# A decode block with grouped attention and a gated layer: the first weight's leading columns are loaded by a transfer of 112 rows and one of 16 rows

## The chip, the cores and the metric

The kernel runs on one core of a Trainium2 chip. A core has five engines with instruction streams of their own (PE or TensorE for matrix products, DVE or VectorE, ACT or ScalarE, POOL or GpSimd, SP or SyncE, which here only issues transfers) and 16 DMA engines that carry the transfers between HBM and the on-chip SBUF. The metric is the device time of one execution in microseconds (us), as a median of several.

## The reference

A layer norm of x, attention of one new token against cached keys and values, a bilinear gated layer, and their product added to x. Cut to what matters:

```python
B, Sq, D = 2, 1, 448
Hq, Hkv, Sk, Dh = 16, 8, 4096, 256      # two query heads share one key/value head
F = 1792

def reference(A_x, A_k_cache, A_v_cache, A_wq, A_wo, B_x, B_w_gate, B_w_up, B_w_down):
    xn = _layernorm(A_x, axis=-1)
    q = (xn @ A_wq).reshape(B, Sq, Hq, Dh).transpose(0, 2, 1, 3)
    k = jnp.repeat(A_k_cache, 2, axis=1)
    v = jnp.repeat(A_v_cache, 2, axis=1)
    p = softmax(jnp.einsum("bhqd,bhkd->bhqk", q, k) * Dh ** -0.5)
    o = jnp.einsum("bhqk,bhkd->bhqd", p, v)
    s = o.transpose(0, 2, 1, 3).reshape(B, Sq, Hq * Dh) @ A_wo
    g = silu((xn @ B_w_gate) * (xn @ B_w_up) @ B_w_down)
    return A_x + s * g
```

All is float32. The caches hold 2 x 8 x 4096 x 256 values each, 134 MB together; the weights add 24 MB. Each byte is read once.

## The kernel before, in words

All inputs are laid out by the host as arrays of 128 rows, one for each SBUF partition, so that each load is one transfer of 128 long rows. `gated_decode_block` keeps three large places in SBUF: a ring of two buffers of 128 x 16384 values (`ring`), and one buffer `slot`. A list `todo`, filled by `plan`, names what is loaded into which place and in which order: w_q's first half (`wq0`, 128 x 7168, into the front of the second ring buffer), the gate and up weights together (`wgu`, first ring buffer), down weights with w_q's second half (`wdq`, slot), the keys of the first pair (`first`, behind wq0 in the second ring buffer), then for each of the 16 pairs of head and batch the values of one pair with the keys of the next (`vk`), `wo` into the slot on the way, and at the end `last0` and `last1`, the second one cut into pieces of 6144, 2048, 2240, 896 and 448 columns. `issue(n)` takes the next n entries of the list and puts one `dma_start` on SP for each piece (`SP.dma_start(t[:, lo:hi], src[:, lo:hi])`, line 272). `issue(4)` at line 291 puts out the first four before anything else.

The order of work on each engine is the order in which the program calls them. A recorder, `Flow`, keeps every call with the boxes of tensors that it reads and writes, and `settle` works out from these which earlier operations it has to wait for; each transfer that somebody waits for has a semaphore of its own. SP works through its transfers in order; a `vk` transfer waits until PE has done with the ring buffer that it overwrites. The two rows of x are loaded by two transfers of one row each on ACT's queue (line 300).

Compute follows the loads: the layer norm of x, `query(0)` (w_q's first half), `ffn_in` (gate and up), `ffn_out` (down), `query(1)`, then a loop over seven pairs of pairs with scores, softmax and values, and an end part in which the last pair is attended, the heads are combined and projected with `wo` and with `wo2`, the three short pieces at the end of `last1` (`project_last`), multiplied by the gate, added to x and stored by one transfer (`res`).

`rows(ps, w, n)` multiplies xn with a folded weight: for k in 0 to 2 and c in 0 to 3 it takes the block of n columns number 4 k + c. For `wq0` n is 512, so that the first four matmuls use columns 0 to 2047, and the others the columns behind.

Of the kernel before, what the change touches and what calls it, by code (L numbers as in the profile page):

```python
# [22 lines left out]
EPS = 1e-5  # L23
WQ = 14 * 512
LEAD = 48


class Flow:
# [115 lines left out]
    def issue(self):  # L144
        nc = self.nc
        lead = nc.alloc_semaphore("lead")
        for _ in range(LEAD):
            nc.vector.sem_inc(lead)
# [72 lines left out]
        return add  # L221


def gated_decode_block(nc, x, first, vk, last0, last1, wq0, wdq, wo, wgu, out):
    flow = Flow(nc)
    PE, DVE, ACT, POOL, SP = [getattr(flow, e) for e in ("PE", "DVE", "ACT", "POOL", "SP")]
    names = iter(range(1000))
# [32 lines left out]
    loaded = {}  # L260
    todo = []

    def issue(n=1):
        for names, place, src, cuts in todo[:n]:
            t = place()
            width = ROW if not names[0].startswith("w") else src.shape[1] // len(names)
            for i, name in enumerate(names):
                loaded[name] = t[:, i * width:(i + 1) * width]
            if names == ["wd", "wq1"]:
                loaded["wd"], loaded["wq1"] = t[:, :14 * D], t[:, 14 * D:]  # L270
            for lo, hi in zip(cuts, cuts[1:]):
                SP.dma_start(t[:, lo:hi], src[:, lo:hi])
        del todo[:n]
# [15 lines left out]
    plan(f"k{LAST + 1} v{LAST}", ring, last0, [0, ROW, 2 * ROW])  # L289
    plan(f"v{LAST + 1} wo2", ring, last1, [0, 6144, ROW, *(ROW + i * D for i in (5, 7, 8))])  # L290
    issue(4)


# [230 lines left out]
    for first in range(0, LAST, B):  # L524
        flow.turn = first
        issue(2)
        if first == 0:
            flow.turn = None
            issue()
            flow.turn = first  # L530
        for i in range(first, first + B):
            p = softmax(i, s)
            o = bank("o")
            values(i, p, o)
            DVE.tensor_copy(ob[:, i % B], o)
            q = copy()
            POOL.tensor_copy(q, query_of(i + 1))
            s = scores(i + 1, q, two())
        total(add_head)
        cb = combine(ob)  # L540
        t = work["h"]()[:, :B * 64]
        DVE.tensor_tensor(t.rearrange("p (s k) -> p s k", s=B), cb.rearrange("p (s k) -> p s k", s=B),
                          over[:, :, None].to_broadcast([128, B, 64]), op=OP.mult)
        turn(oT, first // B, t)
# [19 lines left out]
    t = work["h"]()  # L564
# [62 lines left out]
```

## Time and profile before

| | |
|---|---|
| median of 3 runs | 374.37 us (374.28 to 374.49) |
| the profiled execution's own time | 374.30 us |
| its span in the profile | 372.7 us |
| bytes moved | 158.67 MB, mean 426 GB/s |

The span runs from the first to the last recorded instruction of the profiled execution; 1.6 us of its own time lie around it. In the views below, "SPq" is SP issuing a transfer, PEld the loading of weights into TensorE, and a line like `o<-ring,pT` names what is written and what is read. L220 is the line of the recorder through which nearly all instructions pass, so that operations are told apart by the tensors they touch. A view by stretches gives, for each stretch in us from the span's start, its length, the busy time of PE, PEld, DVE, ACT and POOL with the number of instructions, the granted clock of TensorE, the mean busy share of the 16 DMA engines and the GB/s they moved. A line of a DMA queue gives packets, MB and the share of the 16 engines' time. A line of DMA issues gives the number of issues, KB each and the median time in us from issue to landing. A timeline's line has the start, the duration, the instruction and in brackets how long its engine stood idle before and what ended that.

### The profile page before, as it was taken

The page shows a single profiled execution, that of the slowest core. Times are in us where ns is not written, and L with a number is a line of the kernel's source. Part 1 is how long each engine was busy: PE and PEld are TensorE (multiplying, and loading weights), DVE is VectorE, ACT ScalarE, POOL GpSimd, SP SyncE. Part 2 cuts the span into 40 slices and gives each one's busy share as a digit, 9 for nine tenths or more (in the row PEclk, how much of TensorE's full clock was granted, in tenths as well). Part 3 has the DMA queues.
Part 4 walks back from the last instruction along what each step waited for, and adds up shares of the span by engine and source line. Part 5 has one row for each costly group of instructions (what it writes and reads, how often), then busy time and mean ns, then how long its engine had stood idle before and what let it go on. Part 6 is the DMA issues. An engine that isn't in the chain of part 4 may idle for free. (4 is left out here: it accounts for less than half of the span.)

```text
span 372.7 us, 3346 instructions
## 1 busy us (share of the span) xinstructions
PE 188.0 (50%) x1474; PEld 57.2 (15%) x1474; DVE 75.5 (20%) x124; ACT 26.7 (7%) x44; POOL 5.6 (2%) x28
## 2 busy tenths in 40 slices
PE   0818292171900626555453638271919090908786
PEld 0201020020200201111121102020202030202223
DVE  2101013021130030313031212221131304030430
ACT  1101011001010010101000000101010101010121
POOL 0100000000000000000000000000000000000000
PEclk9968598596875685958595958695867586776999
DMA  8999999999999999999999999999999999999995
GB/s 339 466 424 410 429 433 450 443 445 396 425 459 436 450 443 436 429 394 450 436 450 443 436 429 394 450 436 450 443 436 429 394 450 436 450 397 443 421 414 233
DMA packets 3897, 158.67 MB, mean 426 GB/s; under 512 B 562, under 2 KB 692, under 8 KB 820
## 3 DMA queue, kind: packets, MB, share of 16 engines
q1 hardware_dynamic: 3888, 158.59, 98.6%
q8 instruction: 4, 0.07, 0.1%
q14 instruction: 1, 0.01, 0.0%
q10 hardware_dynamic: 4, 0.00, 0.0%
HBM read 158.54 MB, written 0.06 MB: 426 GB/s over the span
## 5 line engine op out<-in xcount | busy, mean ns | idle before, releaser
L220 PE MATMUL o<-ring,pT 128*32 128x512 f32 x480 | 81.4, 840 | 115.3 <-PEq L172 115.3
L220 PE MATMUL s<-ring,qc 128*32 128x512 f32 x448 | 50.7, 592 | 0.0
L220 PEld LDWEIGHTS o<-ring,pT 128*32 128x32 f32 x480 | 20.7, 149 | 163.5 <-issue 163.5
L220 DVE COPY ob<-o 128x512 f32<-128x512 f32 x14 | 9.7, 692 | 155.9 <-PE o L220 155.9
L220 ACT ACTIVATE p<-s,m 128x1024 f32<-128x1024 f32 x16 | 17.8, 1113 | 287.5 <-DVE m L220 287.5
L220 DVE TENSOR_REDUCE m<-s 128x1 f32<-128x1024 f32 x16 | 19.3, 1205 | 21.9 <-PE s L220 21.9
L220 DVE STREAM_TRANSPOSE pT<-p 128x1024 f32<-128x1024 f32 x15 | 18.7, 1245 | 19.1 <-ACT p L220 19.1
L220 PEld LDWEIGHTS s<-ring,qc 128*32 128x32 f32 x448 | 15.1, 110 | 33.0 <-issue 33.0
L220 PE MATMUL sm<-ident,m 128*1 128x128 f32 x16 | 4.3, 269 | 25.6 <-PEq L172 23.7
L220 PE MATMUL s<-ring,xnT 128*32 128x448 f32 (+1 forms) x72 | 12.1, 828 | 8.3 <-DMA ring<-wgu 8.3
L220 DVE TENSOR_REDUCE mx<-sm 1x128 f32<-1x512 f32 x16 | 10.9, 679 | 8.0 <-PE sm L220 8.0
L220 PE MATMUL sm<-one,mx 1*128 1x1 f32 x16 | 3.2, 198 | 12.9 <-PEq L172 12.1
L220 PE MATMUL s<-slot,hT 128*32 128x448 f32 x28 | 5.4, 885 | 8.0 <-DMA slot<-wdq 8.0
L220 POOL COPY qc<-qT 128x64 f32<-128x64 f32 x14 | 3.2, 236 | 290.9 <-PE s L220 283.6
L220 PE MATMUL s<-ring,qT 128*32 128x512 f32 x64 | 7.5, 597 | 0.0
L220 PEld LDWEIGHTS sm<-ident,m 128*1 128x1 f32 x16 | 1.3, 79 | 35.1 <-issue 32.9
L220 DVE RECIPROCAL over<-sm 128x2 f32<-128x2 f32 x8 | 1.4, 170 | 23.9 <-PE sm L220 23.9
L220 PE MATMUL s<-ident,pT 2*128 2x2 f32 x4 | 0.6, 247 | 10.5 <-DVE pT L220 10.5
L220 PE MATMUL cb<-ob,add_blocks 128*32 128x128 f32 x128 | 5.2, 279 | 0.6 <-ACT ob L220 0.6
L220 PEld LDWEIGHTS s<-ring,xnT 128*32 128x32 f32 x72 | 2.6, 145 | 17.0 <-DMA ring<-wgu 9.2
L220 PE MATMUL s<-ring,oT 128*32 128x112 f32 (+2 forms) x76 | 5.1, 314 | 0.1
L220 PE MATMUL wide<-slot,oT 128*32 128x448 f32 x48 | 4.9, 539 | 0.0
(65 smaller groups left out, 60.9 us busy)
## 6 DMA issues: line engine op xcount, KB each, us to landing
ring<-last SPq DMA_DIRECT2D x2, 4096.0 KB, 26.3
slot<-wdq SPq DMA_DIRECT2D x1, 6720.0 KB, 42.2
ring<-wgu SPq DMA_DIRECT2D x1, 6272.0 KB, 26.0
slot<-wo SPq DMA_DIRECT2D x1, 5376.0 KB, 46.6
ring<-first SPq DMA_DIRECT2D x1, 4096.0 KB, 51.2
ring<-wq SPq DMA_DIRECT2D x1, 3584.0 KB, 11.7
ring<-last SPq DMA_DIRECT2D x1, 3072.0 KB, 21.1
ring<-last SPq DMA_DIRECT2D x1, 1120.0 KB, 23.7
```

Source lines behind the costliest of these rows:

```text
L220: self.flow.record(self.engine, lambda: method(out, *args, **kw), writes, reads, name == "dma_start")
```

## The change

The first 2,048 of wq0's 7,168 columns become two arrays of their own: `wqs` with rows 0 to 111, and `wqx` with rows 112 to 127, stored as 4 groups of 4 rows with an unused fifth row behind each group, which keeps the groups from lying end to end. Three transfers take the place of one: 112 rows of 8,192 bytes, then 16 rows of 8,192 bytes whose source is the 4 x 4 pattern, then 128 rows of the 5,120 columns left. All three go to the places in SBUF where the one transfer went.

```diff
+SHARE = 4
+EACH = 4
+COLS = 2048
...
-def gated_decode_block(nc, x, first, vk, last0, last1, wq0, wdq, wo, wgu, out):
+def gated_decode_block(nc, x, first, vk, last0, last1, wq0, wqs, wqx, wdq, wo, wgu, out):
...
+            if names == ["wq0"]:
+                most = 128 - SHARE * EACH
+                loaded["wq0"] = t[:, :WQ]
+                SP.dma_start(t[:most, :COLS], wqs)
+                SP.dma_start(t[most:, :COLS], wqx[:, :EACH])
+                SP.dma_start(t[:, COLS:WQ], src)
+                continue
...
+    most = 128 - SHARE * EACH
+    wqs = c(wq0[:most, :COLS])
+    wqx = np.zeros((SHARE, EACH + 1, COLS), np.float32)
+    wqx[:, :EACH] = wq0[most:, :COLS].reshape(SHARE, EACH, COLS)
+    wq0 = c(wq0[:, COLS:])
```

On SP, at the head of its queue (each row names the place that is written, the array that is read, and the shape), before:

```order
L220 DMA ring<-wq 128x7168
L220 DMA ring<-wgu 128x12544
L220 DMA slot<-wdq 128x13440
L220 DMA ring<-first 128x8192
L220 DMA ring<-vk 128x16384 x2
```

and now, three lines further down in the file:

```order
L223 DMA ring<-wqs 112x2048
L223 DMA ring<-wqx 16x1x2048
L223 DMA ring<-wq 128x5120
L223 DMA ring<-wgu 128x12544
L223 DMA slot<-wdq 128x13440
L223 DMA ring<-first 128x8192
L223 DMA ring<-vk 128x16384 x2
```

wgu, wdq and first have two more issues ahead of them; all later transfers stand as before.

On PE, from the first matmul of query(0) to the first of ffn_in (xnT and the part of oT named here hold the transposed xn; s0, s1 and so on are semaphores), before:

```order
L220 MATMUL s<-ring,xnT 32x512 [waits s7,s0]
L220 MATMUL s<-ring,xnT 32x512
L220 MATMUL s<-ring,xnT 32x512 [waits s7]
L220 MATMUL s<-ring,xnT 32x512 x9
L220 MATMUL s<-ring,oT 64x512 x2
L220 MATMUL s<-ring,xnT 32x448 [waits s9,s1]
```

and now:

```order
L223 MATMUL s<-ring,xnT 32x512 [waits s9,s1,s0]
L223 MATMUL s<-ring,xnT 32x512
L223 MATMUL s<-ring,xnT 32x512 [waits s9]
L223 MATMUL s<-ring,xnT 32x512
L223 MATMUL s<-ring,xnT 32x512 [waits s2]
L223 MATMUL s<-ring,xnT 32x512 x7
L223 MATMUL s<-ring,oT 64x512 x2
L223 MATMUL s<-ring,xnT 32x448 [waits s11,s3]
```

The first matmul waits for the two small transfers (s0, s1) instead of the whole weight, and the fifth for the rest (s2). The number and order of the matmuls is the same; the numbers of the other semaphores move up by two.

More of the change, by code (lines that the diff above doesn't have):

```diff
@@ L619 @@
     nc = bacc.Bacc("TRN2", target_bir_lowering=False, num_devices=1, dynamic_dma_scratch_size=1024)
-    arrays = dict(x=x, first=first, vk=vk, last0=last[0], last1=last[1], wq0=wq0, wdq=wdq, wo=wo, wgu=wgu)
+    arrays = dict(x=x, first=first, vk=vk, last0=last[0], last1=last[1], wq0=wq0, wqs=wqs, wqx=wqx, wdq=wdq, wo=wo, wgu=wgu)
     args = [nc.dram_tensor(n, a.shape, mybir.dt.from_np(a.dtype), kind="ExternalInput").ap()
```

## The prediction

> **What bounds the kernel now.** I read the page first: span, busy shares, the DMA queues, and the chain that ended last.
>
> ```profile
> span 372.7 us, 3346 instructions
> ...
> PE 188.0 (50%) x1474; PEld 57.2 (15%) x1474; DVE 75.5 (20%) x124; ACT 26.7 (7%) x44; POOL 5.6 (2%) x28
> ...
> q1 hardware_dynamic: 3888, 158.59, 98.6%
> q8 instruction: 4, 0.07, 0.1%
> q14 instruction: 1, 0.01, 0.0%
> q10 hardware_dynamic: 4, 0.00, 0.0%
> ...
> DMA 6%; PE 3%; DVE 0%; issue 0%
> DMA ring<-last 6%; PE o L220 2%; PE s L220 1%; DVE gate L220 0%
> ```
>
> No compute engine is busy for more than half of the span, while the sixteen DMA engines spend 98.6% of it on SP's queue (q1). The kernel is a stream of weights and caches, and it ends when the last piece has come in. The next view is the DMA queue between 60 and 340 us, away from start and end.
>
> ```profile
> q1 hardware_dynamic: 2174, 121.34, 100.0%
> ```
>
> There the engines have no gap: 121.34 MB in 280 us are 433 GB/s, or 27.1 GB/s for each of 16 engines. Such a stream has no meeting point: an engine that loses a microsecond early carries the loss to the end, as long as the next transfer is always issued before the engine needs it. Whether it is, the issue table says.
>
> ```profile
> ring<-wq SPq DMA_DIRECT2D x1, 3584.0 KB, 11.7
> ...
> ring<-vk SPq DMA_DIRECT2D x14, 30.0
> ```
>
> A vk transfer of 8.39 MB takes 19.4 us at 433 GB/s but lands 30.0 us after its issue, so it stands in the queue for some 10.6 us before its turn. An engine may run several microseconds ahead of or behind the others without meeting an empty queue. So the end is not set by the mean of the engines but by the slowest of them, and the stretches at the end show whether they finish together (the columns wanted are the last two: DMA share and GB/s).
>
> ```profile
> 367.00:368.00 1.00, 0.44 (x16) 0.38 (x16) 0.00 (x0) 0.51 (x1) 0.00 (x0) 1.00 0.97 375
> 368.00:368.50 0.50, 0.43 (x17) 0.22 (x13) 0.22 (x1) 0.00 (x0) 0.00 (x0) 1.00 0.50 190
> 368.50:369.00 0.50, 0.50 (x32) 0.50 (x28) 0.09 (x1) 0.00 (x0) 0.00 (x0) 1.00 0.29 115
> 369.00:369.50 0.50, 0.50 (x24) 0.27 (x18) 0.00 (x0) 0.00 (x0) 0.00 (x0) 1.00 0.22 86
> 369.50:370.00 0.50, 0.50 (x20) 0.31 (x21) 0.00 (x0) 0.00 (x0) 0.00 (x0) 1.00 0.00 0
> ```
>
> They do not. All are busy until 368; after 368.5 a share of 0.29, then 0.22, is left: 115 and 86 GB/s are 4.2 and 3.2 engines at 27.1. So about four engines run until about 369.5 and twelve have stopped soon after 368. The three shares times 0.5 us times 16 make 8.1 engine-us after 368.0; four engines up to 369.5 are 6.0 of it, the other twelve share 2.1, so they stop at 368.2 on average, 1.3 us before the late ones.
>
> What made four engines late? Queue q8 has exactly four packets, the fetches of instructions. In the queue's views of 41 to 44 and of 366 to 368 us one of them each stands beside the stream:
>
> ```profile
> q8 instruction: 1, 0.02, 2.0%
> ...
> q8 instruction: 1, 0.02, 2.7%
> ```
>
> 2.0% of 16 engines for 3 us is 0.96 us, 2.7% for 2 us is 0.86: each takes one engine from the stream for 0.9 us, somewhat more with the gaps around it. Had one engine taken all four, it alone would be 3.5 us late; four engines late by 1.3 us each mean that every fetch went to another engine.
>
> Last, does the end follow the late engines? The rows of weight loads of the last matmuls carry their waits:
>
> ```profile
> 368.28 0.92 PEld L220 LDWEIGHTS s<-ring,oT 128*32 128x32 f32 x40 [0.34 <-DMA ring<-last]
> ...
> 369.43 0.35 PEld L220 LDWEIGHTS s<-ring,oT 128*32 128x32 f32 x16 [0.23 <-DMA ring<-last]
> ...
> 369.97 0.16 PEld L220 LDWEIGHTS s<-ring,oT 128*32 128x32 f32 x8 [0.19 <-DMA ring<-last]
> ```
>
> TensorE waits for each of the three last pieces (0.34, 0.23, 0.19 us) and starts on the last at 369.97, some 0.45 us after the DMA share falls to nothing. If all late engines deliver everything earlier by less than 0.3 us, the ends of these waits move by the same amount, and so does the store behind them.
>
> **The change part by part.** *One row's price.* A row of 2,048 columns is 8,192 bytes: at 27.1 GB/s 0.302 us of one engine.
>
> *Who gets how many.* q1's 3,888 packets are 27 transfers of 144: 128 rows and 16 small packets that close it, one per engine; the two one-row loads of x (q10) are 4 packets, one row and one closing packet each. So a 128-row transfer uses all 16 engines, 8 rows each, and a one-row transfer one. The 112 rows divide by 16: 7 rows each, one fewer than before, on every engine. What is left, 16 rows written and 4 groups of 4 read, is a shape the trace does not show. Bounds: 16 engines with a row each (then all is as before, 8 each), or one engine with 16 rows (4.5 us more for it). I take 4 engines with 4 rows, as the 4 groups are the only cut that both sides share without breaking a group; the padding row keeps them apart. Then twelve engines carry 7 rows (-0.302 us) and four "favoured" ones 11 (+0.906 us).
>
> [...]
>
> *More closing packets, smaller packets.* Every engine closes one transfer more, the favoured ones two, and 8 rows of 28,672 bytes become 8,192 and 20,480. Below: nothing. Above: in the five short pieces at the end, between 352 and 367 us, the share stays at 0.96 to 1.00, so five such boundaries cost at most 0.04 of 12 us, 0.1 us each.
>
> ```profile
> 352.00:364.00 12.00, 10.92 (x105) 3.42 (x100) 4.61 (x6) 3.18 (x6) 0.00 (x0) 1.00 0.96 412
> 364.00:367.00 3.00, 2.94 (x36) 0.88 (x28) 0.00 (x0) 0.18 (x1) 0.00 (x0) 1.00 1.00 419
> ```
>
> I take 0.03 us, near the lower end, since from 60 to 340 us fourteen boundaries leave no measurable gap.
>
> *Two more issues on SP.* They go ahead of wgu, wdq and first; the timeline of SP:
>
> ```profile
> 0.74 0.38 SPq L220 DMA_DIRECT2D ring<-wq  x1
> 1.17 0.42 SPq L220 DMA_DIRECT2D ring<-wgu  x1
> 1.64 0.42 SPq L220 DMA_DIRECT2D slot<-wdq  x1
> 2.11 0.68 SPq L220 DMA_DIRECT2D ring<-first  x1
> ```
>
> and the first stretches, with the DMA share before the last column (a packet counts where it starts, hence 3.00):
>
> ```profile
> 0.00:1.50 1.50, 0.00 (x0) 0.00 (x0) 0.00 (x0) 0.00 (x0) 0.78 (x8) 1.00 0.00 0
> 1.50:2.00 0.50, 0.00 (x0) 0.00 (x0) 0.00 (x0) 0.48 (x1) 0.00 (x0) 1.00 3.00 749
> ```
>
> Each issue stands 0.45 us behind the one before, and the packets start between 1.5 and 2.0, so some 1.0 us after the first issue. wgu, wdq and first are issued 0.9 us later, into a queue that then holds 10 us of work and more. The close one is wq's rest: issued at about 1.65, its packets can start at 2.7, while the 112 rows (0.92 MB at 433 GB/s, 2.1 us) keep the engines busy until 3.9. That cover of 1.2 us hides both issues; without it every engine would stand still for what is missing. Price: 0.
>
> *The waits.* TensorE's first wq matmul now waits for wqs and wqx, the fifth for wq's rest. Queued behind are the rest of query(0), its two transposes on DVE, and ffn_in.
>
> ```profile
> 12.71 5.18 PE L220 MATMUL s<-ring,xnT 128*32 128x512 f32 x24
> ...
> 27.22 0.20 PEld L220 LDWEIGHTS s<-ring,xnT 128*32 128x32 f32 x8 [9.21 <-DMA ring<-wgu]
> ```
>
> TensorE stands for 9.2 us before wgu is there, so 0.9 us on wq is hidden. wgu itself also ends 0.9 us later on the favoured engines; ffn_in, and with it the first vk issue at 35.9, move by that, out of the 10.6 us that vk stands in the queue. Price: 0; what would be late next is a vk issue, and it has ten times the room.
>
> *Sum, if no late engine is favoured.* Late engines: -0.302 + 0.03 = -0.27 us, from 369.5 to 369.2. Favoured ones: +0.906 + 0.05 on 368.2, so 369.2 or just under: they draw level. The end moves by -0.27 us. The profiled execution took 374.30 us for its span of 372.7; it becomes 374.03 with a span of 372.4. It lies 0.07 under the median of 374.37, so the forecast is 374.1.
>
> **The rivals.** *A late engine is among the favoured four (slower).* Then that engine gets 0.906 + 0.05 on top of its 369.5, the last piece lands at 370.45, and the time is 374.37 + 0.95 = 375.3. It decides as soon as one of the four fetches goes to one of the four engines. For it: nothing in these rows names the engines; with both fours drawn at random they would miss each other only in 27 of 100 cases (495 of 1,820). Against it: four fetches on four different engines look like a rotation; if they sit side by side in a ring of 16, 9 of the 16 positions miss a fixed block of four.
>
> *The 16 rows go over all 16 engines (nothing changes).* Then each carries 8 rows again and only the closing packets are added: 374.4. For it: 16 rows are written, and all 27 transfers of q1 use 16 engines. Against it: it would have to cut the groups.
>
> [...]
>
> *A gap at the start (slower or level).* If the issue of wqx takes longer than the 0.42 us of its neighbours by more than the 1.2 us of cover, all engines stand. At 1.5 us more the gap is 0.3 us and eats the gain; at 2.5 us more it is 1.3 us, 375.4. For it: its pattern is the only one with a padded source; first took 0.68. Against it: no row near 1.7 us.
>
> **How the numbers follow.** No overlap 0.59, overlap 0.26, all sixteen 0.08, gap 0.07. The first is likeliest: 374.1, its own range 373.85 to 374.35 (favoured engines that start late could take most of the 0.27; a gain over 0.4 has no source). To hold 8 in 10, the range has to take in the overlap at 375.3: 373.85 to 375.4. About 0.2%, 0.75 us, is what a measurement of this kernel can tell from no change: the gain of 0.27 (0.07%) lies inside, and 0.95 (0.25%) just outside. Slower: 0.85 of the overlap and a third of the gap, 0.25. Faster: 0.03. Same: 0.72.
>
> **What would show it.** Four engines: q1 has 3,888 + 128 + 20 = 4,036 packets (4,048 if sixteen, 4,033 if one). No gap: the DMA share between 2 and 12 us is no lower than before. No overlap: the share after 368 stays near 0.5 up to about 369.2 (eight engines) and falls at once, and the last weight loads start near 369.7; overlap shows instead a share of 0.06 to 0.2 lasting to 370.4, and a last start near 370.9. Wrong would be the whole picture if engines meet somewhere, so that early rows don't reach the end, or if fetches move to other engines from run to run.

## The result, and the profile after

The changed kernel takes 376.31 us (median of 6 runs, 376.09 to 376.91) against 374.41 us for the kernel before (374.28 to 374.62): 1.0052 times as long, 95% interval 1.004 to 1.0065. It is 1.9 us slower, where 0.3 us faster was forecast, and lies above the range that was given. Of all executions on record three took far longer than the others of their kernel (961.7 us of the kernel cut only by columns at the start, 963.64 of the kernel before, 418.73 of the last experiment's kernel), and the comparisons leave them out.

The page of the changed kernel, the lines that answer to those of before:

```profile
span 374.5 us, 3348 instructions
...
q1 hardware_dynamic: 4036, 158.59, 98.5%
q8 instruction: 4, 0.07, 0.1%
```

The picture is the same: the stream of transfers is the bound, the bytes are the same, and q1 has exactly the 4,036 packets that were forecast for 16 rows on four DMA engines. The span is 1.8 us longer. Where, is seen at both ends. First SP's timeline and the first microseconds (us from the start, then the columns of the stretches as before, the last one GB/s):

```profile
1.20 0.79 SPq L223 DMA_DIRECT2D ring<-wqx  x1
...
2.04 0.40 SPq L223 DMA_DIRECT2D ring<-wq  x1
```

```profile
4.00:8.00 4.00, 0.00 (x0) 0.00 (x0) 1.81 (x5) 0.00 (x0) 0.00 (x0) 1.00 0.97 281
```

The kernel before moved 431 GB/s in the stretch from 4 to 8 us:

```profile
4.00:8.00 4.00, 0.00 (x0) 0.00 (x0) 0.86 (x3) 0.00 (x0) 0.00 (x0) 1.00 1.00 431
```

The share of busy time is 0.97: the engines are hardly idle, their packets take longer (for 8,192 bytes 0.45 us at the median between 3 and 6.5 us). At 150 GB/s less, 0.60 MB are left undone after 4 us, and at 433 GB/s these are 1.4 us, most of the loss.

The trace also has a record of each packet, with start, duration and bytes, but without the engine. With each packet's bytes spread over its duration, the stream is 0.1 us of data behind the kernel before at 4 us, 1.6 us at 8 us and 1.7 us at 10 us, and it stays there: 1.6 us at 360 us. Then the last stretches:

```profile
369.00:369.50 0.50, 0.02 (x4) 0.02 (x4) 0.00 (x0) 0.42 (x1) 0.00 (x0) 1.00 0.88 337
369.50:370.00 0.50, 0.50 (x16) 0.35 (x16) 0.00 (x0) 0.00 (x0) 0.00 (x0) 1.00 0.58 215
370.00:370.50 0.50, 0.44 (x20) 0.33 (x18) 0.31 (x1) 0.00 (x0) 0.00 (x0) 1.00 0.43 165
370.50:371.00 0.50, 0.50 (x32) 0.50 (x28) 0.01 (x1) 0.00 (x0) 0.00 (x0) 1.00 0.21 79
371.00:371.50 0.50, 0.50 (x28) 0.34 (x21) 0.00 (x0) 0.00 (x0) 0.00 (x0) 1.00 0.09 36
```

The stair is 1.9 us later, and it has more steps than before. The share is 0.88 in the stretch from 369.0 (before, it was 0.50 from 368.0), and the last engine runs until about 371.5. In a steady stream the next packet of an engine starts 3 or 4 ns before the end of the last one, so the records can be followed engine by engine. So read, they show eight engines between 369.1 and 369.8, three of the favoured four at 370.3, the four that lost time to an instruction fetch (0.88 to 1.04 us each on q8) between 370.6 and 371.3, and the fourth favoured one at 371.5. So no fetch fell on a favoured engine; all sixteen are late. The waits of the last weight loads have moved with it, and their form has not changed:

```profile
370.18 0.92 PEld L223 LDWEIGHTS s<-ring,oT 128*32 128x32 f32 x40 [0.32 <-DMA ring<-last]
...
371.81 0.16 PEld L223 LDWEIGHTS s<-ring,oT 128*32 128x32 f32 x8 [0.20 <-DMA ring<-last]
```

From the last wait (371.81) to the end of the span there are 2.7 us, as before (369.97 to 372.7). The loss is in the stream: 1.7 of the 1.8 us are made in the first 10 us, and the rest is in the uneven end.

### The profile page after: what moved, and what is told of

Its sections match the earlier page's. It is cut to its first block, busy times and chain, and to the rows that moved or that the text cites. A ratio compares the mean times of both kernels' runs of the same rounds, so it can differ in the third digit from the quotient of the medians.

```text
span 374.5 us, 3348 instructions
## 1 busy us (share of the span) xinstructions
PE 189.3 (51%) x1474; PEld 57.3 (15%) x1474; DVE 75.5 (20%) x124; ACT 26.8 (7%) x44; POOL 5.6 (1%) x28
## 3 DMA queue, kind: packets, MB, share of 16 engines
q1 hardware_dynamic: 4036, 158.59, 98.5%
## 6 DMA issues: line engine op xcount, KB each, us to landing
ring<-wgu SPq DMA_DIRECT2D x1, 6272.0 KB, 27.3
```

## The experiments

Two theories were set up first, and a third one that needs neither. A: the padded 16-row transfer, with its 0.79 us of issue and its four engines, holds the others up. B: the cut by rows gives the engines other partitions than in the 128-row transfers, and they get in each other's way. C: short rows and more transfers cost by themselves. Later B was split into P, places (the loss comes from which partitions an engine writes), and R, rows (it comes from how many rows an engine gets); both are the author's guesses. The expectations name the kernels by labels: e1_columns, e2_plain16, e3_order and e4_wo are the first four below, f4_columns the fifth, then come f1_halves, f2_sixteens, f3_strided, g2_own, g3_foreign, g1_groups and g4_dose. The text says "behind" for the data, as a time at 433 GB/s, that a stream has moved less than the kernel before, by the packet records.

### Only the cut by columns

```diff
-                SP.dma_start(t[:most, :COLS], wqs)
-                SP.dma_start(t[most:, :COLS], wqx[:, :EACH])
+                SP.dma_start(t[:, :COLS], wqs)
                 SP.dma_start(t[:, COLS:WQ], src)
```

> Only the cut by columns is kept: 128 rows x 2,048 columns, then 128 rows x 5,120; no cut by rows, no padded source. Theories on the 1.9 us: (A) the padded 16-row transfer, issued for 0.79 us on SP and carried by four DMA engines, holds up all engines at the start; (B) the cut into 112 and 16 rows gives the DMA engines other rows than in the 128-row transfers, and they get into each other's way until that has passed; (C) short rows and one more transfer at the start cost by themselves. A and B: 374.4 us, within 0.3 of the kernel before, and packets of normal length (0.31 us for 8,192 bytes) after 3.8 us. C: 375.2 us or more.

Measured: 374.42 us, ratio to before 1.0005 (0.9993 to 1.0017). Its stretch from 4 to 8 us:

```profile
4.00:8.00 4.00, 0.00 (x0) 0.00 (x0) 1.95 (x6) 0.00 (x0) 0.00 (x0) 1.00 1.06 452
```

Rows of 8,192 bytes, one more transfer and one more issue cost nothing that can be measured here. C falls.

### The 16 rows read as plain rows

```diff
-                SP.dma_start(t[most:, :COLS], wqx[:, :EACH])
+                SP.dma_start(t[most:, :COLS], wqx)
...
-    wqx = np.zeros((SHARE, EACH + 1, COLS), np.float32)
-    wqx[:, :EACH] = wq0[most:, :COLS].reshape(SHARE, EACH, COLS)
+    wqx = c(wq0[most:, :COLS])
```

> The cut into 112 and 16 rows stays, but the 16 rows are read as plain rows, so that each of the 16 DMA engines should get one of them (q1 4,048 packets). A: 374.4 us, and an issue of 0.4 us on SP instead of 0.79. B: slow packets between 3 and 8 us remain, 375.5 to 376.3 us. C: as e1 or above.

Measured: 375.95 us, ratio 1.0044 (1.003 to 1.0057); q1 has 4,048 packets. SP issues the 16 rows in 0.42 us instead of 0.79, every engine has 8 rows again, and still:

```profile
4.00:8.00 4.00, 0.00 (x0) 0.00 (x0) 1.36 (x4) 0.00 (x0) 0.00 (x0) 1.00 1.02 275
```

Most of the loss is there without padding and without favoured engines. A falls as the main cause, B stands. Whether the padded form adds to it cannot be told: the intervals of the two kernels overlap.

### The padded transfer behind the rest of wq

```diff
-                SP.dma_start(t[most:, :COLS], wqx[:, :EACH])
                 SP.dma_start(t[:, COLS:WQ], src)
+                SP.dma_start(t[most:, :COLS], wqx[:, :EACH])
```

> All three transfers of the change, but the padded one is issued third, behind the 128 rows x 5,120 columns, which then have their descriptors before the 112 rows have run out. A as a hold-up of the issue alone: the stretch from 5.0 to 6.5 us, where 11 to 15 engines are at work, is filled, and of the 1.9 us about 0.6 comes back (375.7 us). A as a slowing down of all data while the padded transfer is made: the slow packets move to a later place but stay, 376 us. B: slow packets stay, 376.0 us.

Measured: 377.56 us, ratio 1.0074 (1.0057 to 1.009): worse than any theory had it. Two stretches show where:

```profile
4.00:8.00 4.00, 0.00 (x0) 0.00 (x0) 1.82 (x6) 0.00 (x0) 0.00 (x0) 1.00 1.07 400
11.00:17.00 6.00, 0.92 (x5) 0.21 (x8) 0.00 (x0) 0.97 (x4) 0.62 (x3) 1.00 1.14 377
```

The first stretch is less hurt than in the change (400 against 281), but a second slow one has come between 11 and 17 us, when the padded 16 rows run among those of the next 128-row transfer: 377 GB/s where the kernel before has 486:

```profile
11.00:17.00 6.00, 6.00 (x27) 1.41 (x26) 0.80 (x5) 0.97 (x4) 0.70 (x3) 1.00 1.13 486
```

A view by stretches counts a packet where it starts, so where packets are long a single row can be off by 50 to 90 GB/s: the kernel cut only by columns, which loses nothing, has 520 in this stretch. By the packet records the stream of e3_order is 0.7 us behind at 11 us and 2.2 us at 17 us. At the end one of its engines runs alone, 1.4 us after the others; that is where the rest of the 3.1 us comes in, and why this engine is late was not found.

The issues were early enough here, so the hold-up of an issue is not the price; while four engines wrote 16 rows beside a 128-row transfer, the whole stream was slowed (1.5 us more behind at 17 us than at 11).

### The same cut in the middle of the stream

```diff
+            if names == ["wo"]:
+                most = 128 - SHARE * EACH
+                loaded["wo"] = t[:, :LATE * D]
+                SP.dma_start(t[:most, :COLS], wos)
+                SP.dma_start(t[most:, :COLS], wox[:, :EACH])
+                SP.dma_start(t[:, COLS:LATE * D], src)
+                continue
```

> wq0 is loaded as in the kernel before; the same cut (112 rows, 4 x 4 rows padded, the rest) is made in wo, which is issued at 58 us behind two transfers, where the queue has some 10 us of work. If the loss belongs to the start, only the shift of rows is left: twelve engines carry one row less and four three rows more, the four late engines are none of the four (after's end shows that), and the time is 374.1 us (-0.27). If B holds anywhere in the stream, slow packets show behind wo and the time is 375 us or more.

Measured: 378.19 us, ratio 1.0098 (1.0084 to 1.0113), 3.7 us of loss instead of 0.3 of gain. The stretch from 90 to 98 us, in which wo comes:

```profile
90.00:98.00 8.00, 4.17 (x20) 1.12 (x24) 0.00 (x0) 0.00 (x0) 0.00 (x0) 0.50 1.03 275
```

The loss does not need the start; at the start it was even half as large. From here on the tests are made at this place, where the stream is even.

### The control there: only the cut by columns

```diff
+            if names == ["wo"]:
+                loaded["wo"] = t[:, :LATE * D]
+                SP.dma_start(t[:, :COLS], wos)
+                SP.dma_start(t[:, COLS:LATE * D], src)
+                continue
```

> wo's first 2,048 columns come by a transfer of their own, all 128 rows, in the place in the stream where e4_wo made its cut by rows. [...] (R) rows: a transfer whose engines get fewer than 8 rows is slow whichever partitions they are. Both: no slow packets here, 374.4 us, so that e4's 3.7 us belong to the cut by rows and not to the extra transfer.

Measured: 374.47 us, ratio 0.9999 (0.9988 to 1.001).

```profile
90.00:98.00 8.00, 5.65 (x28) 1.58 (x32) 0.00 (x0) 0.00 (x0) 0.00 (x0) 0.50 1.05 449
```

This row is the measure for the next ones: 449 GB/s with all 128 rows, 275 with the cut by rows. The difference over 8 us is 1.39 MB, at 433 GB/s 3.2 of the 3.7 us. The packets say the same: at this place 8,192 bytes take 0.309 us in the control and 0.54 us at the median with the cut by rows.

### Two halves, eight neighbours, eight strided

```diff
-                SP.dma_start(t[:, :COLS], wos)
+                for lo in (0, 64):                                       # halves
+                    SP.dma_start(t[lo:lo + 64, :COLS], wos[lo:lo + 64])
...
+                for lo in range(0, 128, 16):                             # sixteens
+                    SP.dma_start(t[lo:lo + 16, :COLS], wos[lo:lo + 16])
...
+                for lo in range(8):                                      # strided
+                    SP.dma_start(t[lo::8, :COLS], wos[lo * 16:lo * 16 + 16])
```

In the strided kernel the host also puts the rows of wos in this order, and the recorder is told that the eight transfers do not touch each other's rows (not shown).

> The same 2,048 columns of wo as two transfers of rows 0 to 63 and 64 to 127, 4 rows for each engine. [...] R as a matter of an odd count (7 rows): no loss, 374.4. R as a matter of fewer rows: a loss that cannot be told from P here.

> The same columns as eight transfers of 16 neighbouring rows, one row for each engine. [...] R: the same time as f3_strided, which has the same row counts, issues and bytes.

> The same columns as eight transfers of 16 rows, but to every eighth partition instead of 16 neighbours (the source is stored so that each transfer reads 16 rows that follow each other, as in f2_sixteens). [...] R: the same time as f2_sixteens.

Measured: halves 378.70 us, ratio 1.0116 (1.0097 to 1.0134); sixteens 379.59, 1.0134 (1.0116 to 1.0152); strided 378.51, 1.0107 (1.0089 to 1.0126). The same stretch, first of the sixteens (with its first half by itself), then of the strided ones:

```profile
90.00:94.00 4.00, 0.00 (x0) 0.00 (x0) 0.00 (x0) 0.00 (x0) 0.00 (x0) 0.50 0.96 176
...
90.00:98.00 8.00, 2.71 (x16) 0.85 (x20) 0.00 (x0) 0.00 (x0) 0.00 (x0) 0.50 1.07 215
```

```profile
90.00:98.00 8.00, 3.28 (x16) 0.92 (x20) 0.00 (x0) 0.00 (x0) 0.00 (x0) 0.50 1.01 256
```

The four microseconds in which the halves come, alone:

```profile
90.00:94.00 4.00, 0.00 (x0) 0.00 (x0) 0.00 (x0) 0.00 (x0) 0.00 (x0) 0.50 0.96 213
```

The halves run at 213 GB/s (218 from 91 to 93 us by the packet records), about half of the stream's 433. Four rows for each engine are as bad as seven (378.70 us against 378.19 in e4_wo), so it is not the odd count. Sixteens and strided have the same issues, rows and bytes and differ in the partitions that a transfer writes; every run of the strided kernel (377.91 to 378.81) was faster than every run of the other (378.93 to 379.71). R has the same time for both, so places have a part in it: 4.1 against 5.2 us of loss. By the packet records halves and strided rows end up equally far behind, 3.5 us each, and the neighbours 5.1 us. Whether R has a part was left open by these three.

### Own and foreign places

A transfer of 16 rows whose values are not used is added ahead of wo, once at partitions 0 to 15 and once at 112 to 127. One small DVE copy near the end reads a column of it; all else is the kernel before. If places matter, as P has it, the two times differ; the names own and foreign are the author's, and no record names the engines that write a partition.

```diff
+LO = 0            # own; 112 in the other kernel
...
+                more = t[:, LATE * D:LATE * D + COLS]
+                SP.dma_start(more[LO:LO + 16], wox[:, :4])
```

> The kernel before with one more transfer ahead of wo, whose values are not used: 16 rows of 8,192 bytes from a padded 4 x 4 source, into columns of the slot that are free, at partitions 0 to 15. [...] R (rows, or the padded form as such): slow packets as in e3_order behind its padded transfer, 376 us or more, and the same time as g3_foreign.

> As g2_own, same source, same four engines, same bytes, but at partitions 112 to 127, the place where the change puts its 16 rows. [...] R: the same time as g2_own.

Measured: own 374.78 us, ratio 1.0013 (1.0003 to 1.0024); foreign 376.45, 1.006 (1.0036 to 1.0084). Own, then foreign, in the four microseconds of this transfer:

```profile
90.00:94.00 4.00, 1.79 (x12) 0.57 (x16) 0.00 (x0) 0.00 (x0) 0.00 (x0) 0.50 1.07 461
```

```profile
90.00:94.00 4.00, 0.25 (x4) 0.23 (x8) 0.00 (x0) 0.00 (x0) 0.00 (x0) 0.50 0.88 269
```

Same bytes, same padded source, same 0.79 us of issue: 461 GB/s at one place, 269 at the other. The form of the transfer costs nothing: own is 0.3 us slower by the medians, and 131 kB more at 433 GB/s are 0.3 us. Its packets of 8,192 bytes all take 0.309 us, and none of the packets around them is longer than usual. In the foreign run every one of the sixteen engines loses 1.3 to 1.9 us to longer packets. So what costs is the place. It is not a slow place as such, since the 128-row transfers write the same partitions at full rate (433 GB/s between 60 and 340 us); that it costs because other engines write these partitions in the transfers around it is the author's reading under P, which no record shows.

### All 128 rows from a source in 16 groups

```diff
-                SP.dma_start(t[:, :COLS], wos)
+                SP.dma_start(t[:, :COLS], wos[:, :8])
...
-    wos = c(wo[:, :COLS])
+    wos = np.zeros((16, 9, COLS), np.float32)
+    wos[:, :8] = wo[:, :COLS].reshape(16, 8, COLS)
```

> wo's first 2,048 columns as one transfer of all 128 rows from a source padded in 16 groups of 8 rows: 16 engines, 8 rows each, as in a plain transfer, and no cut by rows. If such a source gives an engine 8 neighbouring partitions where a plain transfer gives it others, P says slow packets and 376 to 379 us although every engine has its 8 rows; R says 374.4. If the engines get the same partitions either way, both say 374.4 and the run does not tell.

Measured: 378.34 us, ratio 1.0102 (1.0084 to 1.012).

```profile
90.00:94.00 4.00, 0.00 (x0) 0.00 (x0) 0.00 (x0) 0.00 (x0) 0.00 (x0) 0.50 0.89 190
```

One transfer, 128 rows, 16 engines with 8 rows each, q1 with the 4,032 packets of the control, and the loss is 3.9 us. R falls. Two things can differ between this kernel and the control at 374.47 us: the gaps in the source, and the division of partitions among the engines. Gaps cost nothing in the own-place run, where four engines read a source of the same kind, so the division is what is left. This is an inference: no record names the partitions that an engine writes.

### A quarter of the bytes

```diff
-COLS = 2048
+COLS = 512
```

> e4_wo (cut of wo into 112 rows and 4 x 4 rows) with 512 columns instead of 2,048, a quarter of the bytes that go through the cut. P: the loss is the time in which bytes go to foreign places, so about a quarter of 3.7 us: 375.3 us, slow packets for some 2 us instead of 8. If the loss were a fixed price of the form, 378 us again.

Measured (the cut of wo into 112 and 4 x 4 rows): 375.51 us as the median of five runs, ratio 1.003 (1.0016 to 1.0045), 1.0 us of loss. For a quarter of the bytes that is 0.28 of e4_wo's 3.7 us; by the packet records 1.1 of 3.3 us are lost at this place, a third. The loss goes with the bytes, with at most some 0.3 us of a part that does not.

## Why the prediction was wrong, point by point

**The bound and the end: right.** DMA is the bound (q1 98.5% of 16 engines' span), engines carried a loss from the start to the end, TensorE follows the last piece (a wait of 0.20 us for it at 371.81). What was lost by 10 us (1.7 us by the packet records) was still there at 360 us (1.6).

**Who gets how many rows: right.** 4,036 packets say four engines for these 16 rows from 4 groups, and 4,048 say sixteen for the plain rows. That the groups set the number was the author's estimate, which these two counts fit; what sets it was not shown, and no record names an engine.

**"One row's price": here the prediction failed.** It took 0.302 us for a row of 8,192 bytes from the rate between 60 and 340 us, where only 128-row transfers run, and used it for transfers of 112 and of 16 rows. It asked how many rows an engine gets, and never which partitions. What the runs showed in its place: between 3 and 6.5 us packets of 8,192 bytes took 0.45 us at the median in the changed kernel and 0.309 in the kernel cut only by columns, and the rows of 20,480 bytes behind them, from 5 to 7.5 us, 1.12 instead of 0.76. The price of a row thus rose for all sixteen engines, and for the 128-row transfer next to the cut as well. The sum had -0.302 us for the late engines; the runs showed +1.9 at the start and +3.7 in the middle of the stream. The term "more closing packets, smaller packets", 0.03 us, was right as it stood: the cut by columns costs nothing.

**Places: a term that the sum did not have.** The halves ran at 213 GB/s, about half of the stream's 433. The 16 neighbours had 176 in the first four microseconds and, by the packet records, 156 from 93.9 to 95 us, when no engine is in a 128-row transfer. With 16 added rows from one and the same form of source the stream moved 461 GB/s when they went to partitions 0 to 15, and 269 when they went to 112 to 127. What sets these rates, no run shows. The cut into two halves was a loss: 378.70 us against 374.47 for one transfer of the same bytes.

**Two more issues on SP: not quite free.** The price was put at 0. The padded transfer is issued in 0.79 us instead of 0.42, and the rest of wq starts late enough that, by the packet records, only 11 to 14 of the 16 engines are at work between 5.2 and 6.2 us, a loss of some 0.2 us. But the plain rows were issued in 0.42 us, kept all 16 engines at work there and lost as much within the interval, so this is not what the 1.9 us are.

**The waits: right that they cost nothing, too small in size.** wgu lands 2.6 us later than before (2.48 + 27.3 = 29.8 against 1.17 + 26.0 = 27.2), ffn_in follows, the first vk issue goes from 35.9 to 38.2 (0.9 us was forecast for both), and all of that stays under the 10.6 us of queue.

**The rival with the other sign: wrong as well.** It had 375.3 us for a fetch on a favoured engine. By the packet records no fetch fell on one. The kernel is slower for a reason that no rival had.

**What stays open.** If the added rows of the foreign run had stopped the four engines that carry them and left the other twelve at 27.1 GB/s each, the rate would be 325 GB/s, an estimate from the stream's 433; the run had 269, and every engine lost about as much as those four (1.3 to 1.9 us each). So engines that carry none of these rows are slowed too, and why was not found. Nor was it settled why the loss at the start is half of that in the middle of the stream, where the same bytes go through the same cut.

No version beat the kernel before. The idea of the change, to take rows from engines that fetch instructions, was not to be had in this way: a row taken from an engine has to be written by another one, and even a quarter of the bytes lost 1.0 us for a gain of less than 0.1.

## What to carry to other kernels

Do not cut a stream of 128-row transfers by rows: each of the cuts tried (112 + 16, 64 + 64, 8 x 16, or 128 rows in padded groups) cost some 1.4 to 5 us per megabyte, while a cut by columns was free (374.42 and 374.47 us). When the price of a transfer is read from a trace, ask of the row whether its transfers have the same rows, places and form of source as the new one: here the 433 GB/s of 128 plain rows did not hold for 112 and 16 of them (281). A DMA share near 1 with fewer GB/s than elsewhere (0.97 at 281) meant longer packets here (0.45 us at the median instead of 0.309 for 8,192 bytes), not idle engines, and the view by stretches shows both numbers in one line.

## What the runs showed of the hardware that was not expected

The shape of the source alone changed the rate, by the inference above through which engine writes which partition, which no record names: 128 rows from plain memory ran at 449 GB/s in the stretch of 8 us, the same 128 rows from 16 groups with a gap behind each at 244:

```profile
90.00:98.00 8.00, 2.99 (x16) 0.90 (x20) 0.00 (x0) 0.00 (x0) 0.00 (x0) 0.50 0.99 244
```

And 131 kB written by four engines to partitions 112 to 127 instead of 0 to 15 took the whole stream of sixteen from 461 to 269 GB/s for four microseconds, 2 us of loss for a transfer whose bytes are worth 0.3, shared by all sixteen engines.
